# Pooled attention with a gated convolutional layer on one core: exponentials per head, division in two steps, two transposes of x by DMA, two conv quarters by taps, and a new order

## The chip, the core and the metric

The kernel runs on one core of a Trainium2 chip. Five engines work from queues of their own, each in order, and wait for each other by semaphores: TensorE (PE: matrix products and transposes), VectorE (DVE), ScalarE (ACT), GpSimd (POOL) and SyncE (SP, which here only starts transfers). Tensors lie in SBUF, on 128 partitions; products land in PSUM, which has eight banks of 512 fp32 values per partition. The metric is the device time of one execution in microseconds, lower is better.

## What is computed

q, k and v have 8 sequences, 8 heads, 576 positions and 64 values per head. Keys and values are averaged over 8 neighbouring positions, which leaves 72 per head; attention over these gives x, 576 x 512 per sequence. Then a layer with 1024 inner channels, a convolution of width 3 along the positions as the gate, and an output product:

```python
def _attn_ref(q, k, v):
    k_p = k.reshape(B, H, Sp, pool, D).mean(axis=3)
    v_p = v.reshape(B, H, Sp, pool, D).mean(axis=3)
    scores = scale * np.matmul(q, k_p.transpose(0, 1, 3, 2))
    scores = scores - np.max(scores, axis=-1, keepdims=True)
    attn = np.exp(scores)
    attn = attn / (np.sum(attn, axis=-1, keepdims=True) + 1e-09)
    return np.matmul(attn, v_p).astype(np.float32)

def _moe_ref(x, w_in, conv_w, w_out):
    h = np.maximum(x @ w_in, 0.0)
    ...
    for k in range(K):
        conv_out += conv_w[k][None, None, :] * hp[:, k:k + S, :]
    gate = 1.0 / (1.0 + np.exp(-conv_out))
    return (h * gate @ w_out).astype(np.float32)
```

The subtraction is of the maximum of each position and head, so it is one number per partition for each block of 72 scores.

## The kernel before

**Tiles.** Two sequences form a group (0 to 3). A group's 1152 positions make nine tiles of 128 (group 0: ten, since its sequences are kept apart), 37 in all. A tile (g, t) goes through one chain of operations, written in `add_att` (L1193):

- `att_scores` (TensorE): the scores of 8 heads, 8 x 72 columns, into two PSUM banks. The ring "s" has two slots, so at most two tiles' scores stand at once.
- `att_max` (VectorE, L608): the negated maximum per position and head, 8 columns "negm".
- `att_shift`: for groups 1 to 3 VectorE adds the negated maximum to all 576 scores and writes "sd" in SBUF (L620); for group 0 (`SHIFT_PE`) TensorE adds it within PSUM (L628). With that the scores' banks are free in groups 1 to 3.
- `att_exp` (ScalarE, L646): one exponential over all 576 columns, with the scale 1/64 for the mean over 8 and the root of 64.
- The exponentials "e" are transposed to "eT": by TensorE and a copy (`att_turn`, L657, `att_copy`, L671) in groups 0 and 1, by a DMA that SP starts (`att_send`, L666) in groups 2 and 3.
- `att_values` (TensorE, L682): products with the pooled values and a column that gives the sum.
- `att_divide` (VectorE): a reciprocal of the 8 sums (L695) and one multiplication over 512 columns (L697), which gives "x".
- x is transposed to "xT": for sequences below `X_DMA` by TensorE and a copy (`att_turn_out`, L714, `att_copy_out`, L722), for the others by a DMA that SP starts (`att_out`, L706).

**The layer** of a sequence b is `add_ffn` (L1246): for each of 8 blocks of 128 inner channels `ffn_in` (TensorE, L727, two halves of four matmuls into two PSUM banks) and `ffn_relu` (ScalarE, L736), which frees them. The convolution runs by groups of four blocks, (b, f4) with f4 = 0 or 1, which are called quarters here as in the change (a quarter of the two sequences of a group). Normally a quarter is two `ffn_conv` of two blocks on TensorE with diagonal weights (L889), four tanh on ScalarE (L914), `ffn_gate` (L925, L927) and a multiplication with h (`ffn_times`, L935) on VectorE. A sequence in `WRAP` has its ends copied by GpSimd first (`ffn_wrap`, L811 and L812), and an `ffn_conv` of it has 24 matmuls, else 32. For a quarter in `TAPS` no matmul is made: per block ScalarE multiplies h by the middle tap's weight, a scale per partition (L862), VectorE adds the two other taps (L864), ScalarE takes the tanh (L869), and `ffn_tap_gate` (L875, L876) gates all four blocks. The output products are `ffn_out` (TensorE, L943), a copy (`ffn_copy`, L954) and a store (`ffn_store`, L966).

**The order.** Every operation is listed once with its engines and a booked cost; the table `ORDER` gives the sequence in which they are issued. An entry n stands for operation n // 2, on its first engine if n is even and on its second if odd; -1 is a filler matmul at the start. `FORMS` and `PLACES` give the form of some products and the PSUM banks. So nothing is decided at run time: each engine works its list from top to bottom, and what stands behind a waiting operation waits too.

Of the kernel before, what the change touches and what calls it, by code (L numbers as in the profile page):

```python
# [33 lines left out]
class Graph:  # L34
# [20 lines left out]
    X_DMA = 4  # L55
# [3 lines left out]
    WRAP = (4, 5, 6, 7)  # L59
    TAPS = ((4, 1), (5, 0), (5, 1), (6, 0), (6, 1), (7, 0))  # L60
# [6 lines left out]
    SHIFT_PE = ((0, 0), (0, 1), (0, 2), (0, 3), (0, 4), (0, 5), (0, 6), (0, 7), (0, 8), (0, 9))  # L67
    TURN_DMA = 2
    BANKS = 8
    ORDER = (  # L70
# [52 lines left out]
    )  # L123
    FORMS = (
        1, 0, 1, 0, 1, 1, 1, 0, 0, 0, 0, 1, 1, 0, 0, 1, 1, 0, 0, 0, 0, 1, 1, 0, 0, 0, 0, 1, 0, 0, 0, 1, 1, 1, 1, 0, 1, 1, 1, 1,
    )
    PLACES = (
# [50 lines left out]
def kernel(  # L178
# [73 lines left out]
    def buf(*key):  # L252
        return buffers[key[0]][tokens[key].slots[0]]
# [1165 lines left out]
```

## Time and profile before

| | |
|---|---|
| median of 3 runs | 217.81 us (217.51 to 218.0) |
| span of the profiled execution, first to last instruction | 216.5 us |
| mean granted TensorE clock | 0.992 |
| data moved | 33.46 MB, mean 155 GB/s |
| DMA issued by SP for x (L706) / for e (L666) | 18 / 18 |

In the views an engine is PE, PEld (weight loads), DVE, ACT or POOL, and L12 is line 12 of the kernel. A group's row gives the operation, the tile written and read, shapes, count, then after the first bar the busy time in us and the mean of one in ns, and after the second the idle time before it with what ended it. Busy time of an engine counts overlapped stretches once: consecutive operations of ScalarE overlap at their ends, so a mean is longer than the distance between two starts. In a timeline or a chain the first number is the start, the second the length, both in us.

### The profile page before, as it was taken

How to read it: one execution, taken by the hardware profiler on the slowest of the kernel's cores; microseconds unless marked ns; L12 is line 12 of the kernel's file. 1: busy time of each engine (PE TensorE's matmuls, PEld its weight loads, DVE VectorE, ACT ScalarE, POOL GpSimd, SP SyncE). 2: the span in 40 equal slices, each digit the busy share in tenths (PEclk: the TensorE clock that was granted, in tenths of full speed). 3: DMA queues.
4: the chain of work that ended last, by engine and by line, in shares of the span. 5: the costliest groups of instructions: out<-in, count | busy, mean ns of one | idle time of the engine just before them, and what ended most of it. 6: DMA issues, size and time to landing. Idle time of an engine off the chain costs nothing.

```text
span 216.5 us, 6617 instructions
## 1 busy us (share of the span) xinstructions
PE 201.9 (93%) x2753; PEld 137.0 (63%) x2753; DVE 193.2 (89%) x334; ACT 162.7 (75%) x278; POOL 41.5 (19%) x78
## 2 busy tenths in 40 slices
PE   7599999969999999999999899989999999999992
PEld 3557778855788776766776675665656666654451
DVE  7598989999999999999999799999899999998621
ACT  2548885896998887787497594878979999997420
POOL 8644330050052101000000030002201210370000
PEclk9799999999999999999999999999999999999999
DMA  6999999999999999969687634576347745602685
GB/s 210 227 207 209 206 207 208 210 205 206 207 205 206 154 153 179 158 164 165 131 111 100 136 74 89 58 156 148 78 104 153 158 100 123 145 0 51 169 242 171
DMA packets 48833, 33.46 MB, mean 155 GB/s; under 512 B 28300, under 2 KB 43812, under 8 KB 48804
## 3 DMA queue, kind: packets, MB, share of 16 engines
q0 software_dynamic: 15216, 15.40, 43.5%
q1 hardware_dynamic: 32512, 16.13, 36.6%
q10 hardware_dynamic: 1076, 1.52, 2.5%
q8 instruction: 21, 0.34, 0.7%
q14 instruction: 8, 0.07, 0.1%
HBM read 32.52 MB, written 9.44 MB: 194 GB/s over the span
## 4 chain that ended last, share of the span: by engine, by line
PE 45%; DVE 34%; issue 6%; ACT 6%; DMA 5%; SPq 2%; DVEq 0%
PE psum L943 20%; PE psum L727 16%; DVE negm L608 7%; DVE x L697 6%; DVE sd L620 4%; DVE gT L935 4%; DMA hT<-in_k_dram 3%; DVE v L486 3%; DVE gT L927 3%; PE psum L889 2%; DMA out_dram<-osb 2%; DVE r L695 2%; PE psum L682 2%; ACT e L646 2%; DVE gT L925 1%
## 5 line engine op out<-in xcount | busy, mean ns | idle before, releaser
L727 PE MATMUL psum<-xT,w_in_sb 128*128 128x288 bf16 x512 | 74.1, 286 | 2.2 <-DMA xT<-x 1.1
L943 PE MATMUL psum<-w_out_sb,gT 128*128 128x512 bf16 (+1 forms) x296 | 69.5, 374 | 0.7 <-DVE gT L935 0.6
L727 PEld LDWEIGHTS <-w_in_sb 128*128 128x128 bf16 x512 | 47.9, 98 | 19.1 <-issue 2.0
L736 ACT ACTIVATE hT<-psum 128x576 bf16<-128x576 f32 x64 | 40.3, 650 | 14.0 <-PE psum L727 13.4
L943 PEld LDWEIGHTS <-gT 128*128 128x128 bf16 x296 | 27.3, 98 | 26.5 <-issue 0.9
L864 DVE SCALAR_TENSOR_TENSOR tg<-hT,convw,tg 128x576 f32<-128x576 bf16 x48 | 37.6, 815 | 0.5
L608 DVE TENSOR_REDUCE negm<-psum 128x8 f32<-128x576 f32 (+2 forms) x37 | 27.5, 752 | 2.3 <-PE psum L582 1.6
L697 DVE TENSOR_TENSOR x<-psum,r 128x512 bf16<-128x512 f32 (+1 forms) x37 | 25.6, 691 | 1.4
L811 POOL COPY hT<-hT 128x126 bf16<-128x126 bf16 x16 | 7.5, 467 | 97.6 <-ACT hT L736 80.1
L620 DVE TENSOR_TENSOR sd<-psum,negm 128x576 f32<-128x576 f32 x27 | 20.2, 753 | 0.5
L682 PE MATMUL psum<-vm,eT 128*128 128x130 bf16 (+5 forms) x240 | 18.9, 222 | 1.1 <-DVE x L697 0.7
L646 ACT ACTIVATE e<-sd 128x576 bf16<-128x576 f32 x27 | 18.2, 685 | 1.3 <-DVE sd L620 1.1
L954 ACT COPY osb<-psum 128x512 f32<-128x512 f32 x27 | 15.7, 585 | 4.4 <-PE psum L943 4.2
L889 PE MATMUL psum<-hT,dw 64*64 64x288 bf16 (+2 forms) x608 | 18.7, 261 | 0.1
L682 PEld LDWEIGHTS <-eT 128*128 128x128 bf16 (+1 forms) x240 | 15.3, 100 | 5.4 <-DMA eT<-e 1.2
L862 ACT ACTIVATE tg<-hT,convw 128x576 f32<-128x576 bf16 x24 | 18.1, 772 | 0.1
L889 PEld LDWEIGHTS <-dw 64*64 64x64 bf16 x608 | 14.8, 107 | 4.6 <-issue 3.7
L869 ACT ACTIVATE gT<-tg 128x576 bf16<-128x576 f32 x24 | 16.3, 683 | 0.7 <-DVE tg L864 0.5
L914 ACT ACTIVATE gT<-psum 128x576 bf16<-128x576 f32 x20 | 12.9, 651 | 3.9 <-PE psum L889 2.7
L914 ACT ACTIVATE tg<-psum 128x576 bf16<-128x576 f32 x20 | 13.0, 652 | 2.6 <-PE psum L889 1.4
L935 DVE TENSOR_TENSOR gT<-gT,hT 128x2304 bf16<-128x2304 bf16 x10 | 13.5, 1352 | 0.1
L486 DVE TENSOR_TENSOR v<-v 128x1280 bf16<-128x1280 bf16 (+2 forms) x24 | 13.0, 540 | 0.2
(84 smaller groups left out, 234.2 us busy)
## 6 DMA issues: line engine op xcount, KB each, us to landing
out_dram<-osb SPq DMA_DIRECT2D x54, 128.0 KB, 2.4
v<-in_v_dram POOLq DMA_DIRECT2D x8, 512.0 KB, 13.1
qp<-in_q_dram POOLq DMA_DIRECT2D x7, 576.0 KB, 14.4
kk<-in_k_dram POOLq DMA_DIRECT2D x3, 1152.0 KB, 14.6
out_dram<-qp ACTq DMA_DIRECT2D x10, 128.0 KB, 2.7
hT<-in_k_dram SPq DMA_DIRECT2D x2, 576.0 KB, 5.0
w_in_sb<-in_moe_w_in_dram POOLq DMA_DIRECT2D x2, 512.0 KB, 14.2
w_out_sb<-in_moe_w_out_dram POOLq DMA_DIRECT2D x1, 1024.0 KB, 24.7
```

Of the source, the lines that this page charges most:

```text
L608: nc.vector.tensor_reduce(out=a["m"][0:rows], in_=a["s"][0:rows, :, 0:2 * KW].rearrange("p a (h s) -> p a h s", s=Sp), axis=AX.X, op=OP.ma ...
L620: nc.vector.tensor_tensor(out=a["d"][0:rows], in0=a["s"][0:rows, :, 0:2 * KW].rearrange("p a (h s) -> p a h s", s=Sp), in1=a["m"][0:rows]. ...
L646: nc.scalar.activation(out=dst, in_=src, func=ACT.Exp, scale=1.0 / (POOL * 8.0),)
L682: nc.tensor.matmul(out=a["o"][lo:hi, h // 4, (h % 4) * (D + 1):(h % 4 + x1 - x0) * (D + 1)], lhsT=a["eT"][:, j, lo:hi], rhs=buf("vm", b)[: ...
L697: nc.vector.tensor_tensor(out=a["x"][0:rows].rearrange("p (a h d) -> p a h d", a=2, d=D), in0=ov[:, :, :, 0:D], in1=r[0:rows].unsqueeze(3) ...
L727: nc.tensor.matmul(out=banks(ps)[:, j, 0:SC], lhsT=w_in_block(dc, fb), rhs=buf("xT", g)[:, dc, i * S + j * SC:i * S + (j + 1) * SC], start ...
L736: nc.scalar.activation(out=h_of(b)[:, fb].rearrange("p (a s) -> p a s", a=2), in_=banks(ps)[:, :, 0:SC], func=ACT.Relu, scale=0.5,)
L864: nc.vector.scalar_tensor_tensor(out=acc, in0=h, scalar=w, in1=acc, op0=OP.mult, op1=OP.add)
L889: nc.tensor.matmul(out=banks(pss[r ^ c])[c * D:(c + 1) * D, j, lo:hi], lhsT=dw[r * D:(r + 1) * D, tap * n_fb + fb, :], rhs=hT[r * D:(r + 1 ...
L914: nc.scalar.activation(out=t.rearrange("p (a s) -> p a s", a=2), in_=banks(ps)[:, :, 0:SC], func=ACT.Tanh, scale=0.5,)
L935: nc.vector.tensor_tensor(out=gate, in0=gate, in1=h_of(b)[:, four], op=OP.mult)
L943: nc.tensor.matmul(out=bank(ps)[0:rows, columns], lhsT=buf("gT", g)[:, fb, t * P:t * P + rows], rhs=w_out_sb[:, fb, columns], start=(fb == 0),
```

## The change

- `EIGHT` lists all 27 tiles of groups 1 to 3. For these `att_shift` is left out, and `att_exp` issues eight activations, one per head, which read the 72 scores in PSUM and add the head's negated maximum as a bias per partition. The scale goes into the pooling matrix and the identity with which keys are turned (`KSCALE`), so `att_exp` has no scale any more.
- `att_divide` becomes `att_invert` (reciprocal, VectorE) and `att_divide` on either engine: one multiplication on VectorE, or eight activations with a scale per partition on ScalarE. In the new order 9 of 37 are on ScalarE: (0,2), (0,4), (1,3), (1,7), (2,1), (2,8), (3,1), (3,5), (3,6).
- `X_DMA` = 2: the nine tiles of group 1 have x transposed by DMA.
- `TAPS` gains (4,0) and (3,1); `WRAP` gains sequence 3. The gate of a taps quarter is listed as two operations.
- The late output buffers of group 3 wait for the q transfers of sequences 4 to 7, not for 7 alone.
- `ORDER`, `FORMS` and `PLACES` are new throughout. In the counts: copies of xT 15 on ScalarE and 4 on VectorE become 8 and 2; eT 16 and 3 become 12 and 7; whole-tile output copies 32 and 3 become 27 and 8; qT 7 and 7 become 9 and 5.

```diff
-    X_DMA = 4
+    X_DMA = 2
...
-    WRAP = (4, 5, 6, 7)
-    TAPS = ((4, 1), (5, 0), (5, 1), (6, 0), (6, 1), (7, 0))
+    WRAP = (3, 4, 5, 6, 7)
+    TAPS = ((4, 0), (4, 1), (5, 0), (5, 1), (6, 0), (6, 1), (7, 0), (3, 1))
...
+    KSCALE = 1.0 / (POOL * 8.0)
...
+    def by_head(g, t):
+        return (g, t) in Graph.EIGHT
...
-        nc.vector.memset(pm[0:TB, :, 0:Sp], 1.0)
+        nc.vector.memset(pm[0:TB, :, 0:Sp], KSCALE)
...
+        nc.vector.tensor_scalar(out=ident_k, in0=ident, scalar1=KSCALE, scalar2=None, op0=OP.mult)
...
+        if by_head(g, t):
+            for n in range(H):
+                r, k = n // 4, n % 4
+                at = (k // 2 * 4 + r * 2 + k % 2 if a["by_rows"] else n) * Sp
+                nc.scalar.activation(
+                    out=e[0:rows, at:at + Sp],
+                    in_=a["s"][0:rows, r, k * Sp:(k + 1) * Sp],
+                    func=ACT.Exp,
+                    bias=a["m"][0:rows, r, k:k + 1],
+                )
+            return
...
-            scale=1.0 / (POOL * 8.0),
...
+    def att_invert(g, t):
+        nc.vector.reciprocal(out=buf("r", g, t)[0:rows_of(g, t)], in_=att_heads(g, t)[:, :, :, D])
+
+    def att_divide(g, t, engine):
...
+        if engine == "ACT":
+            for n in range(H):
+                nc.scalar.activation(
+                    out=a["x"][0:rows, n * D:(n + 1) * D],
+                    in_=ov[:, n // 4, n % 4, 0:D],
+                    func=ACT.Identity,
+                    scale=r[0:rows, n // 4, n % 4:n % 4 + 1],
+                )
+            return
...
+        if by_head(g, t):
+            o = add({"ACT": 0.9}, key, lambda: att_exp(g, t), after=[o], uses=[e, s, ng, lim])
+        elif shift_by_dve(g, t):
...
-        o = add(dve(0.2, 0.69), key, lambda: att_divide(g, t), after=[o], uses=[x, rr, big])
+        o = add({"DVE": 0.115}, key, lambda: att_invert(g, t), after=[o], uses=[rr, big])
+        o = add({"DVE": 0.61, "ACT": 0.82}, key, None, after=[o], uses=[x, rr, big])
+        o.emit = lambda o=o: att_divide(g, t, o.engine)
```

More of the change, by code (lines that the diff above doesn't have):

```diff
@@ L67 @@
     SHIFT_PE = ((0, 0), (0, 1), (0, 2), (0, 3), (0, 4), (0, 5), (0, 6), (0, 7), (0, 8), (0, 9))
+    EIGHT = ((1, 0), (1, 1), (1, 2), (1, 3), (1, 4), (1, 5), (1, 6), (1, 7), (1, 8), (2, 0), (2, 1), (2, 2), (2, 3), (2, 4), (2, 5), (2, 6), (2, 7), (2, 8), (3, 0), (3, 1), (3, 2), (3, 3), (3, 4), (3, 5), (3, 6), (3, 7), (3, 8))
     TURN_DMA = 2
@@ L70 @@
     ORDER = (
[52 rows of a table removed]
[54 rows of a table added]
     )
     FORMS = (
-        1, 0, 1, 0, 1, 1, 1, 0, 0, 0, 0, 1, 1, 0, 0, 1, 1, 0, 0, 0, 0, 1, 1, 0, 0, 0, 0, 1, 0, 0, 0, 1, 1, 1, 1, 0, 1, 1, 1, 1,
+        0, 0, 1, 1, 1, 1, 1, 1, 1, 1, 1, 1, 0, 1, 1, 1, 1, 0, 0, 1, 0, 0, 0, 0, 0, 0, 1, 1, 0, 0, 0, 1, 1, 1, 1, 1, 1, 0, 1, 0,
     )
     PLACES = (
[17 rows of a table removed]
[16 rows of a table added]
     )
@@ L224 @@
     ident = const.tile([P, P], BF16, name="ident")
+    ident_k = const.tile([P, P], BF16, name="ident_k")
     mask = const.tile([P, NJ, 3], BF16, name="mask")
@@ L375, in build_pick @@
                     out=pick[:, hh].rearrange("p (s f a e) -> p s f a e", s=2, f=2, a=2)[:, :, f],
-                    in_=ident.rearrange("p (s a hh f e) -> p s a hh f e", s=2, a=2, hh=2, f=2)[:, :, :, hh, f],
+                    in_=ident_k.rearrange("p (s a hh f e) -> p s a hh f e", s=2, a=2, hh=2, f=2)[:, :, :, hh, f],
                 )
@@ L470, in turn_keys @@
                     lhsT=buf("kk", g)[:, c, 0:D],
-                    rhs=ident[:, i * D:(i + 1) * D],
+                    rhs=ident_k[:, i * D:(i + 1) * D],
                     start=True,
@@ L689, in att_values, with att_heads @@
                 )
-    def att_divide(g, t):
+    def att_heads(g, t):
+        return att[g, t]["o"][0:rows_of(g, t), :, 0:4 * (D + 1)].rearrange("p a (h d) -> p a h d", d=D + 1)
+    def att_invert(g, t):
+        nc.vector.reciprocal(out=buf("r", g, t)[0:rows_of(g, t)], in_=att_heads(g, t)[:, :, :, D])
+    def att_divide(g, t, engine):
         a, rows = att[g, t], rows_of(g, t)
-        ov = a["o"][0:rows, :, 0:4 * (D + 1)].rearrange("p a (h d) -> p a h d", d=D + 1)
-        r = buf("r", g, t)
-        nc.vector.reciprocal(out=r[0:rows], in_=ov[:, :, :, D])
+        ov, r = att_heads(g, t), buf("r", g, t)
         a["x"] = buf("x", g, t)
+        if engine == "ACT":
[7 more added lines that the diff above has]
+            return
         nc.vector.tensor_tensor(
@@ L872, in ffn_tap_gate @@
         g, i = where[b]
-        four = slice(4 * f4, 4 * f4 + 4)
-        gate = buf("gT", g)[:, four, i * S:(i + 1) * S]
+        gate = buf("gT", g)[:, 4 * f4:4 * f4 + 4, i * S:(i + 1) * S]
         nc.vector.tensor_scalar(out=gate, in0=gate, scalar1=1.0, scalar2=None, op0=OP.add)
-        nc.vector.tensor_tensor(out=gate, in0=gate, in1=h_of(b)[:, four], op=OP.mult)
     def ffn_conv(b, f2, pss):
@@ L1113, in add_pair @@
             t = token("ps", n=2)
-            o = add({"PE": 0.26}, key, lambda b=b, t=t: turn_keys(b, t), after=[prev, c0], uses=[t, kk[g]], mode=HALF, count=36)
+            o = add({"PE": 0.26}, key, lambda b=b, t=t: turn_keys(b, t), after=[prev, picked], uses=[t, kk[g]], mode=HALF, count=36)
             c = add(either(0.76, 0.71), key, None, after=[o], uses=[t, ktok[b]])
@@ L1209, in add_att @@
         o = add(dve(0.75), key, lambda: att_max(g, t), after=[o], uses=[ng, s])
-        if shift_by_dve(g, t):
+        if by_head(g, t):
+            o = add({"ACT": 0.9}, key, lambda: att_exp(g, t), after=[o], uses=[e, s, ng, lim])
+        elif shift_by_dve(g, t):
             sd = token("sd", g, t)
@@ L1292, in add_ffn @@
                 tanh.append(add(act(0.65 if Graph.ACC < 2 else 0.683), w, lambda fb=fb, ps=ps: ffn_tap_tanh(b, fb, ps), after=[o], uses=[ps, gtok[g]]))
-            gated = add(dve(0.78, 1.39), w, lambda f4=f4: ffn_tap_gate(b, f4), after=tanh, uses=[htok[b], gtok[g]])
+            o = add(dve(0.78), w, lambda f4=f4: ffn_tap_gate(b, f4), after=tanh, uses=[gtok[g]])
+            gated = add(dve(1.39), w, lambda f4=f4: ffn_times(b, f4), after=[o], uses=[htok[b], gtok[g]])
             gdone.setdefault(b, []).append(gated)
@@ L1326, in add_ffn @@
             if f2 % 2 and cross:
-                gated = add(dve(0.78, 1.39), w + 6 * f2 + Graph.GATE, lambda f4=f4: ffn_tap_gate(b, f4), after=tanh[f4], uses=[htok[b], gtok[g]])
+                o = add(dve(0.78), w + 6 * f2 + Graph.GATE, lambda f4=f4: ffn_tap_gate(b, f4), after=tanh[f4], uses=[gtok[g]])
+                gated = add(dve(1.39), w + 6 * f2 + Graph.GATE, lambda f4=f4: ffn_times(b, f4), after=[o], uses=[htok[b], gtok[g]])
                 gdone.setdefault(b, []).append(gated)
@@ L1340, in add_out @@
             key += nudge("ot", 9 * g + t)
-            osb, free = (token("late", g, t), qdone[7, 0]) if g == 3 else (token("osb", g, t), [])
+            osb, free = (token("late", g, t), [x for n in range(4, B) for x in qdone[n, 0]]) if g == 3 else (token("osb", g, t), [])
             need = [a for x in groups[g][0:i + 1] for a in gdone[x]]
```

139 rows, old and new, of tables (ORDER, PLACES) are left out of this document.

## The prediction

> **What bounds the kernel now.** I read the summary first, then the busy time by stretches, then the chain of work that ended last, and only then the groups and the timeline of ScalarE. Summary and chain by engine, from the page:
>
> ```profile
> span 216.5 us, 6617 instructions
> ...
> PE 201.9 (93%) x2753; PEld 137.0 (63%) x2753; DVE 193.2 (89%) x334; ACT 162.7 (75%) x278; POOL 41.5 (19%) x78
> ...
> PE 45%; DVE 34%; issue 6%; ACT 6%; DMA 5%; SPq 2%; DVEq 0%
> ```
>
> The same by stretches of the span (length, then busy time of PE, PEld, DVE, ACT, POOL, then clock, DMA share, GB/s):
>
> ```profile
> 0.00:20.00 20.00, 15.66 (x251) 10.21 (x252) 14.81 (x44) 10.50 (x18) 12.06 (x27) 0.91 1.05 213
> 20.00:50.00 30.00, 27.44 (x553) 21.87 (x554) 28.10 (x51) 23.51 (x40) 7.53 (x11) 1.00 1.23 207
> 50.00:144.00 94.00, 91.24 (x1461) 65.49 (x1457) 90.75 (x158) 74.36 (x128) 9.67 (x17) 1.00 0.89 147
> 144.00:200.00 56.00, 55.33 (x442) 33.42 (x442) 53.55 (x74) 50.25 (x86) 12.28 (x24) 1.00 0.49 108
> 200.00:216.50 16.50, 12.25 (x65) 6.04 (x63) 5.93 (x10) 4.05 (x8) 0.00 (x0) 1.00 0.68 191
> ```
>
> And pieces of the chain that ended last (start, length, what):
>
> ```profile
> 31.02 0.63 PE psum L657 x10
> ...
> 82.91 0.74 PE psum L889 x32
> ...
> 91.75 0.76 DVE sd L620
> ...
> 93.07 0.68 DVE negm L608
> ...
> 162.07 1.96 PE psum L727 x16
> 164.03 0.86 PE psum L943 x4
> ...
> 195.55 0.86 PE psum L889 x24
> ...
> 199.10 13.16 PE psum L943 x68
> ```
>
> TensorE and VectorE share the bound: the chain is mostly VectorE up to about 144 us and TensorE alone after it. ScalarE is third. Its idle time is 54 us, but not all of it is usable: 9.5 us lies in the first 20 us (20 - 10.50) and 12.45 us after 200 us (16.5 - 4.05), where the last output matmuls run. That leaves some 32 us, and only 20.6 us of it lies between 50 and 144 us (94 - 74.36).
>
> **The change, part by part.** Groups of instructions with their mean (busy us, mean ns):
>
> ```profile
> L620 DVE TENSOR_TENSOR sd<-psum,negm 128x576 f32<-128x576 f32 x27 | 20.2, 753 | 0.5
> L646 ACT ACTIVATE e<-sd 128x576 bf16<-128x576 f32 x27 | 18.2, 685 | 1.3 <-DVE sd L620 1.1 <-ACT osb L954 0.2
> L727 PE MATMUL psum<-xT,w_in_sb 128*128 128x288 bf16 x512 | 74.1, 286 | 2.2 <-DMA xT<-x 1.1 <-ACT tg L914 0.3 <-ACT gT L914 0.3
> L736 ACT ACTIVATE hT<-psum 128x576 bf16<-128x576 f32 x64 | 40.3, 650 | 14.0 <-PE psum L727 13.4
> L697 DVE TENSOR_TENSOR x<-psum,r 128x512 bf16<-128x512 f32 x35 | 24.2, 692 | 1.3
> L864 DVE SCALAR_TENSOR_TENSOR tg<-hT,convw,tg 128x576 f32<-128x576 bf16 x48 | 37.6, 815 | 0.5
> L954 ACT COPY osb<-psum 128x512 f32<-128x512 f32 x27 | 15.7, 585 | 4.4 <-PE psum L943 4.2
> L722 ACT COPY xT<-psum 128x512 bf16<-128x512 bf16 x13 | 7.6, 591 | 1.0 <-PE psum L714 0.6 <-DVE r L695 0.4
> L722 ACT COPY xT<-psum 128x256 bf16<-128x256 bf16 x2 | 0.7, 371 | 0.0
> L671 ACT COPY eT<-psum 128x640 bf16<-128x640 bf16 x14 | 9.5, 696 | 1.6 <-PE psum L657 1.5
> L534 ACT COPY qT<-psum 128x1152 bf16<-128x1152 bf16 x5 | 5.5, 1124 | 1.7 <-PE psum L520 1.7
> L671 DVE COPY eT<-psum 128x640 bf16<-128x640 bf16 x3 | 1.5, 484 | 0.4 <-ACT kT L431 0.4
> L954 DVE COPY qp<-psum 128x512 f32<-128x512 f32 x3 | 2.1, 689 | 6.0 <-PE psum L943 6.0
> L534 DVE COPY qT<-psum 128x1152 bf16<-128x1152 bf16 x5 | 3.8, 758 | 1.3 <-PE psum L520 1.3
> L927 DVE TENSOR_SCALAR gT<-tg 64x1152 bf16<-64x1152 bf16 x20 | 9.7, 485 | 0.3
> L925 DVE TENSOR_SCALAR gT<-gT 128x1152 bf16<-128x1152 bf16 x10 | 5.4, 542 | 0.0
> L875 DVE TENSOR_SCALAR gT<-gT 128x2304 bf16<-128x2304 bf16 x6 | 4.6, 772 | 0.9 <-ACT gT L869 0.9
> ```
>
> The term that decides is **one short biased ScalarE operation**; the trace has none of 72 columns. So I take it apart by the timeline of ScalarE (start, length of the merged piece, what):
>
> ```profile
> 74.19 1.61 ACT L458 CAST kT<-psum 64x288 bf16<-64x288 f32 x4
> ...
> 153.62 1.74 ACT L736 ACTIVATE hT<-psum 128x576 bf16<-128x576 f32 x3 [0.40 <-PE psum L727]
> ...
> 169.66 1.05 ACT L954 COPY osb<-psum 128x512 f32<-128x512 f32 x2
> ...
> 177.07 0.68 ACT L869 ACTIVATE gT<-tg 128x576 bf16<-128x576 f32 x1
> 177.64 1.43 ACT L862 ACTIVATE tg<-hT,convw 128x576 f32<-128x576 bf16 x2
> 178.97 0.67 ACT L869 ACTIVATE gT<-tg 128x576 bf16<-128x576 f32 x1
> ```
>
> - Slope: (591 - 371)/256 columns of L722 = 0.86 ns per column; I use 0.84, since from there to L671's 640 columns it is (696 - 591)/128 = 0.82. 72 columns take 0.060 us, 64 take 0.054.
> - Start to start from PSUM: three ReLUs (L736) in 1.74 us, the last 0.65 long, are 0.545 apart; less 504 columns (0.423) a 72-column operation would start every 0.122 us.
> - A per-partition operand: L862 reads its scale from a column of convw, L869 does not. 177.07 to 177.64 is 0.57; the two L862 start (178.97 - 177.64)/2 = 0.665 apart. So **0.095 us per operation goes to the operand, and 480 ns of streaming in the operation before did not hide it**.
>
> One biased exponential: 0.122 + 0.095 = 0.217 us; eight of them 1.74 us per tile in place of 0.57 (an exponential of 0.685 with its end overlapped, as L869). One 64-column division: 0.210; eight 1.68 us. Bounds: below, the operand hidden and the overhead of the two L954 copies, (1.05 - 0.585) = 0.465 less 440 columns (0.370) = 0.095, so 0.76 per tile and 0.70 per division; above, the four L458 casts, which hardly overlap: 0.405 apart, less 216 columns (0.181) and with the operand 0.319, so 2.55 and 2.5. I take 0.217: exponential and ReLU are the same kind, from PSUM to bf16.
>
> The Trainium skill, "ScalarE: Activation LUTs", section "What ACT_TABLE_LOAD costs", speaks against the change more strongly: 186 ns plus 0.833 ns per column, about 93 ns more per [128,1] operand, and 93 ns of overlap back to back. By it, as an estimate, an exponential starts every 0.247 us and the ScalarE total below would be 9 us higher; the operand's 0.095 of this trace agrees with it.
>
> ScalarE's queue, from 162.7 us:
> - 27 tiles of groups 1 to 3 (EIGHT): 27 x (1.74 - 0.57) = **+31.6**.
> - 9 divisions that the new ORDER gives to ScalarE (odd entries; seven of them in groups 1 to 3): 9 x 1.68 = **+15.1**. The other 28 stay on VectorE.
> - Quarters (4,0) and (3,1) by taps: 8 L862 of 0.665 = +5.3; their eight tanh move from PSUM to SBUF, +0.2.
> - Copies, each its mean less about 0.11 of overlap: xT 15 to 8 (-3.3), eT 16 to 12 (-2.3), output 32 to 27 (-2.4); qT 7 to 9 (+1.5, one of them short), start-up casts and kT about -0.6. Together -7.1.
>
> Sum 162.7 + 31.6 + 15.1 + 5.5 - 7.1 = **207.8 us**; 172.5 with the low bound, 237 with the high one.
>
> VectorE: 27 shifts -20.3, 9 multiplications -6.2, 16 taps +13.0, two gates 2 x (0.772 - 0.542 - 2 x 0.485) = -1.5, copies (eT +4, output +5, qT -2, xT -2) about +3: **-12 us**, to 181. The reciprocal is the same work in an instruction of its own. TensorE: 36 transposes of x at 0.063 (L657 is such a transpose: 10 in 0.63) -2.3; four conv pairs, two at 0.86 (24 matmuls) and two at 0.74 (32), -3.2; (3,0) goes from the 32 to the 24 form, +0.2: **-5.3 us**. GpSimd gets four more wraps and is 19% busy: cover ample, and without cover a wrap would hold the taps of its two blocks. The scaling moved into the pool matrix and the identities costs one small VectorE operation in the first microseconds: nothing.
>
> What is queued behind: ScalarE takes its list in order. Behind each train of eight stand ReLUs, which free the PSUM pairs of ffn_in; tanh and taps, which VectorE waits for; and, where ScalarE divides, the train waits for VectorE's reciprocal with all of that behind it. The scores' two PSUM banks, free before when the shift had read them, are held now until the eighth exponential, and at most two tiles are allowed (ring "s"). So a late ScalarE stops TensorE.
>
> **Sum.** The eight-fold trains begin with group 1, near 50 us, so the first 20 us and the run of output matmuls at the end keep their ScalarE idle time: 207.8 + 9.5 + 12.45 = **229.8 us** of span with no idle anywhere between. That is a floor for this price (20 to 50 us has 6.5 us of idle today, not all of which can be filled), while overlap at the ends of trains can give a little back; I keep it. The three runs' median 217.81 lies 1.3 us over the profiled span of 216.5, so **231 us**. By high and low neighbours of 0.217 (0.19 to 0.25, 288 operations): -7.8 to +9.5, so 223 to 240.
>
> **Rivals.**
> - *The short operations pack like copies, operand hidden: faster.* Place: the trains in ScalarE's queue; price 0.095 us per operation, ScalarE 172.5 us (80%), no bound. Then TensorE decides: its 5.3 us go, and of the 6.0 us that it idles from 20 to 200 us (180 - 174.0) perhaps 1.2, since VectorE has 12 us less: 216.5 - 6.5 + 1.3 = **211.3 us**. It decides below the price at which ScalarE just fits: (207.8 - (216.5 - 21.95))/288 = 0.046 less, with 3 us of idle left 0.057 less, so **0.16 us per operation**. For it: the two L954 copies come back to back at an overhead 0.027 us less than the ReLUs; the diff's own table books the eight at 0.9 us, which is a booking and no measurement. Against it: the L862 rows.
> - *Between:* at about 0.16 the gain on TensorE and the loss on ScalarE meet: **217 us**, same.
> - *Transposes by DMA come late.* Nine transfers of x join SP's queue between 50 and 100 us, where the engines' share is 0.89 against 0.49 later, ahead of stores and of the eT transfers. eT shows what late means:
>
> ```profile
> DMA to landing us min/median/max: 2.6/2.6/8.3
> ```
>
>   Sequences 3 and 2 would each wait once the 5.7 us of the worst over the median; on top of the fast case 211.3 + 11.4 = **223 us**. For it: L727 did wait for xT; against: it waited 1.1 us in all, with eighteen such transfers there already.
> - *Trains without any overlap* (0.319, as the casts): 237 + 22 + 1.3 = **261 us**. Against: those casts write half the partitions each; all else on ScalarE overlaps.
>
> **Chances.** ScalarE bound at 0.19 to 0.25: 0.50, 231 us, own range 223 to 240. Short operations packed: 0.36. Between: 0.05. Late DMA: 0.04. No overlap: 0.05. Range 209 to 239, which takes in both chief cases; they lie 20 us apart because one unmeasured price decides. What can be told from no change is about 0.2%: faster 0.38, same 0.03, slower 0.59.
>
> **What would show it.** Right: ScalarE above 95% busy between 50 and 170 us, the eight exponentials of a tile 0.2 us or more apart, TensorE idle before ffn_in with ScalarE as releaser, VectorE's busy time near 181 us. Wrong: exponentials starting every 0.1 to 0.15 us, ScalarE near 80% and TensorE over 94% busy.

## The result, and the profile after

The changed kernel is slower: ratio 1.1475 to the kernel before, 95% interval 1.1398 to 1.1553. Four runs gave 248.3, 251.02, 252.91 and 253.79 us (median 251.97) beside 217.66 us for the kernel before (217.51 to 218.0). The two highest of the four count as slow runs and are not in the ratio, so below **249.7 us**, the mean of the other two, stands for the changed kernel, and for u2 and u6, too, the time given is a single run, the faster of two, while the profile is that of the slower. The profiled execution of the changed kernel took 248.3 us, with a span of 246.6.

Summary, clock by slices and chain by engine, from its page:

```profile
span 246.6 us, 6716 instructions
...
PE 209.2 (85%) x2649; PEld 135.8 (55%) x2649; DVE 184.8 (75%) x317; ACT 202.8 (82%) x532; POOL 47.1 (19%) x86
...
PEclk9999999999998579996899999999999999999996
...
ACT 40%; PE 29%; DVE 15%; DMA 6%; issue 6%; SPq 1%; DVEq 0%; ACTq 0%
```

The chain has moved from PE and DVE (45 and 34% before) to ScalarE: 6% became 40%. But ScalarE's 202.8 us are 44 us less than the span. Where it idles is in the same stretches as before (length, busy time of PE, PEld, DVE, ACT, POOL, clock, DMA share, GB/s):

```profile
0.00:20.00 20.00, 13.76 (x238) 8.35 (x239) 14.84 (x45) 10.25 (x19) 9.47 (x20) 1.00 1.05 208
20.00:50.00 30.00, 27.51 (x620) 21.52 (x618) 24.76 (x48) 25.89 (x56) 8.31 (x15) 1.00 1.23 207
50.00:144.00 94.00, 80.11 (x1102) 54.53 (x1102) 66.58 (x115) 81.38 (x251) 12.78 (x22) 0.91 0.91 137
144.00:200.00 56.00, 48.54 (x431) 29.26 (x430) 45.89 (x70) 55.74 (x162) 6.42 (x16) 1.00 0.51 97
200.00:230.00 30.00, 28.84 (x209) 16.87 (x209) 28.50 (x38) 27.30 (x47) 10.12 (x14) 1.00 0.43 97
230.00:246.60 16.60, 10.49 (x56) 5.28 (x54) 4.23 (x6) 2.24 (x4) 0.00 (x0) 0.87 0.68 184
```

From 144 to 200 us ScalarE is busy 55.74 of 56 us: there it is the bound, as forecast. From 50 to 144 us **no engine** is: PE 80, ACT 81 and DVE 67 of 94 us. The rows of the new instructions, by shape:

```profile
L653 ACT ACTIVATE e<-psum,negm 128x72 bf16<-128x72 f32 x216 | 49.5, 414 | 2.0 <-DVE negm L616 2.0
L767 ACT ACTIVATE hT<-psum 128x576 bf16<-128x576 f32 x64 | 42.7, 711 | 5.6 <-PE psum L758 5.4
...
L721 ACT ACTIVATE x<-psum,r 128x64 bf16<-128x64 f32 x64 | 14.3, 382 | 3.3 <-DVE tg L895 2.1 <-DMA xT<-x 0.7 <-DVE r L713 0.5
```

A mean of 414 ns isn't the price of one: consecutive operations overlap, and single records run from 301 to 693 ns. The price is the distance of starts, on ScalarE's timeline:

```profile
69.18 1.74 ACT L721 ACTIVATE x<-psum,r 128x64 bf16<-128x64 f32 x8
70.76 0.70 ACT L767 ACTIVATE hT<-psum 128x576 bf16<-128x576 f32 x1
...
157.81 1.80 ACT L653 ACTIVATE e<-psum,negm 128x72 bf16<-128x72 f32 x8
159.45 0.64 ACT L983 COPY osb<-psum 128x512 f32<-128x512 f32 x1
```

Eight exponentials hold the queue for 159.45 - 157.81 = 1.64 us, **0.205 us each** (forecast 0.217); eight divisions for 1.58 us (forecast 1.68). Then the chain, where the stretch from 50 to 144 us lost time:

```profile
69.14 0.56 DVE x L728
69.72 8.78 DMA xT<-x
78.59 0.70 DVE x L728
...
88.55 3.79 PE psum L758 x16
...
103.96 4.06 DMA xT<-x
```

The transposes of x, now DMAs here, stand in it with 8.78 + 4.06 = 12.8 us; the exponentials (L653) have about 25% of the chain in this stretch, nearly twice as much. At 78.59 us VectorE's next division (L728) had waited until a DMA had read the buffer of an earlier x. What VectorE idled for this is less than the chain shows, since it had other work meanwhile: two such waits, 5.6 us in all. From issue to landing the 27 transfers of x took (first line), and the seven that were issued from 65 to 85 us, where the DMA share was about 1.2 (second line):

```profile
DMA to landing us min/median/max: 2.4/3.0/10.7
...
DMA to landing us min/median/max: 4.6/9.0/10.7
```

SP's queue was held by them, and then by a transfer of q, as its timeline shows (start, length):

```profile
65.59 20.33 SPq L737 DMA_TRANSPOSE xT<-x  x7
86.02 11.37 SPq L536 DMA_TRANSPOSE qT<-qp  x1
```

The 16 matmuls at 88.55 us took 0.237 us each; before, 16 took 1.96 us (162.07 us of the chain before), 0.1225 each. The granted clock is lower there, in two stretches of 20 us:

```profile
80.00:100.00 20.00, 17.00 (x189) 11.12 (x186) 12.86 (x24) 14.79 (x47) 1.77 (x2) 0.78 1.10 154
100.00:120.00 20.00, 16.62 (x234) 9.89 (x235) 14.31 (x23) 16.25 (x48) 5.05 (x10) 0.83 0.67 99
```

### The profile page after: what moved, and what is told of

Read it like the earlier page. It is cut to its first block, busy times and chain, and to the rows that moved or that the text cites. A ratio compares the mean times of both kernels' runs of the same rounds, so it can differ in the third digit from the quotient of the medians.

```text
span 246.6 us, 6716 instructions
## 1 busy us (share of the span) xinstructions
PE 209.2 (85%) x2649; PEld 135.8 (55%) x2649; DVE 184.8 (75%) x317; ACT 202.8 (82%) x532; POOL 47.1 (19%) x86
## 4 chain that ended last, share of the span: by engine, by line
ACT 40%; PE 29%; DVE 15%; DMA 6%; issue 6%; SPq 1%; DVEq 0%; ACTq 0%
ACT e L653 15%; PE psum L972 8%; PE psum L758 8%; DVE tg L895 6%; ACT hT L767 6%; DMA xT<-x 5%; ACT x L721 5%; PE psum L918 3%; ACT tg L893 3%; ACT gT L900 3%; ACT osb L983 2%; PE psum L700 2%; DVE gT L964 2%; PE psum L407 2%; DVE negm L616 2%
## 5 line engine op out<-in xcount | busy, mean ns | idle before, releaser
L895 DVE SCALAR_TENSOR_TENSOR tg<-hT,convw,tg 128x576 f32<-128x576 bf16 x64 | 50.1, 817 | 6.1 <-ACT tg L893 5.7
L653 ACT ACTIVATE e<-psum,negm 128x72 bf16<-128x72 f32 x216 | 49.5, 414 | 2.0 <-DVE negm L616 2.0
L767 ACT ACTIVATE hT<-psum 128x576 bf16<-128x576 f32 x64 | 42.7, 711 | 5.6 <-PE psum L758 5.4
L616 DVE TENSOR_REDUCE negm<-psum 128x8 f32<-128x576 f32 (+2 forms) x37 | 27.5, 755 | 14.8 <-PE psum L603 8.3
L700 PE MATMUL psum<-vm,eT 128*128 128x65 bf16 (+5 forms) x240 | 20.8, 230 | 6.2 <-ACT eT L689 3.2
L893 ACT ACTIVATE tg<-hT,convw 128x576 f32<-128x576 bf16 x32 | 25.6, 816 | 0.5
L728 DVE TENSOR_TENSOR x<-psum,r 128x512 bf16<-128x512 f32 (+1 forms) x28 | 19.1, 685 | 6.2 <-DMA xT<-x 5.6
L700 PEld LDWEIGHTS <-eT 128*128 128x128 bf16 (+1 forms) x240 | 16.4, 105 | 12.2 <-issue 5.3
L900 ACT ACTIVATE gT<-tg 128x576 bf16<-128x576 f32 x32 | 22.8, 726 | 0.0
L964 DVE TENSOR_TENSOR gT<-gT,hT 128x2304 bf16<-128x2304 bf16 x16 | 21.8, 1365 | 0.3
L721 ACT ACTIVATE x<-psum,r 128x64 bf16<-128x64 f32 (+1 forms) x72 | 16.0, 374 | 3.5 <-DVE tg L895 2.1
L713 DVE RECIPROCAL r<-psum 128x8 f32<-128x8 f32 (+1 forms) x37 | 7.5, 204 | 13.9 <-PE psum L700 7.6
L943 ACT ACTIVATE tg<-psum 128x576 bf16<-128x576 f32 x16 | 10.6, 663 | 3.7 <-PE psum L918 3.1
```

The costliest lines, as they stand in the source:

```text
L616: nc.vector.tensor_reduce(out=a["m"][0:rows], in_=a["s"][0:rows, :, 0:2 * KW].rearrange("p a (h s) -> p a h s", s=Sp), axis=AX.X, op=OP.ma ...
L653: nc.scalar.activation(out=e[0:rows, at:at + Sp], in_=a["s"][0:rows, r, k * Sp:(k + 1) * Sp], func=ACT.Exp, bias=a["m"][0:rows, r, k:k + 1],)
L700: nc.tensor.matmul(out=a["o"][lo:hi, h // 4, (h % 4) * (D + 1):(h % 4 + x1 - x0) * (D + 1)], lhsT=a["eT"][:, j, lo:hi], rhs=buf("vm", b)[: ...
L721: nc.scalar.activation(out=a["x"][0:rows, n * D:(n + 1) * D], in_=ov[:, n // 4, n % 4, 0:D], func=ACT.Identity, scale=r[0:rows, n // 4, n ...
L767: nc.scalar.activation(out=h_of(b)[:, fb].rearrange("p (a s) -> p a s", a=2), in_=banks(ps)[:, :, 0:SC], func=ACT.Relu, scale=0.5,)
L893: nc.scalar.activation(out=acc, in_=h, func=ACT.Identity, scale=w)
```

## The experiments

Theory A: ScalarE's added time is the loss, paid in full at the forecast price. Rival B: late transposes of x and a starved TensorE make the rest. Theory C in the expectations of u1 to u3 is TensorE's lower clock. Ratios are to the kernel before, run alongside (217.3 to 218.3 us); line numbers of a variant are its own. A letter u is a part undone in the changed kernel, v and x the kernel before with something put in, w the kernel before with VectorE relieved.

### Undoing one part

**u1**: all divisions on VectorE.

```diff
-        o.emit = lambda o=o: att_divide(g, t, o.engine)
+        o.emit = lambda o=o: att_divide(g, t, "DVE")
```

> The changed kernel with its nine ScalarE divisions back on VectorE. Theory A (ScalarE is the bound and its trains of eight set the price): ScalarE's busy time falls from 202.8 by 9 x 1.68 = 15 us, VectorE's rises by 6 us to 191, and the time falls by 8 to 15 us to 233 to 240 us. Theory B (the transposes of x by DMA in group 1 decide, VectorE and ScalarE wait for their buffers): the 12.8 us of DMA in the chain stay, and the time falls by less than 5 us, 243 us or more. Theory C (the lower granted clock of TensorE between 60 and 120 us decides): no change within 3 us.

240.56 us, ratio 1.1039 [1.0942, 1.1136]: 9 us back for 13.2 us of ScalarE (202.8 to 189.6 busy).

**u2**: the shift on VectorE again, right behind the maximum, and one exponential of 576 columns.

```diff
+        if by_head(g, t):
+            a["d"] = buffers["sd"][len(shifted) % 3]
+            shifted.append((g, t))
+            nc.vector.tensor_tensor(
...
+                op=OP.add,
+            )
...
-        if by_head(g, t):
+        if False:
```

> The changed kernel with the eight exponentials of groups 1 to 3 undone: VectorE shifts directly behind the maximum, one exponential per tile. Theory A: ScalarE loses 27 x 1.17 = 31 us (to 171), VectorE gains 20 us (to 205) and becomes the bound with TensorE: 220 to 230 us. Theory B: the late transposes stay, 235 us or more. Theory C: 245 us.

243.18 us; a miss. ScalarE fell to 176.1 us busy and VectorE rose to 201.8, and only 6.5 us came back. This alone does not show that ScalarE is not all of the loss: in the profile of this run ScalarE waits 17.2 us, 16 times, for the new shift, so VectorE took over a part of it.

**u3**: six of group 1's nine x tiles get buffers of their own (the unused "sd"), so that their divisions do not wait for a DMA to read an old x.

```diff
-        a["x"] = buf("x", g, t)
+        a["x"] = x_own[t] if g == 1 and t < 6 else buf("x", g, t)
```

> The changed kernel with six of the nine x tiles of group 1 in buffers of their own (the space of the shifted scores, unused there), so that no division waits for a transfer of an earlier x. Theory A alone: 245 to 250 us, the waits of VectorE for the transfer of xT (5.6 us) go and come back as waits for ScalarE. Theory B: the chain loses its 12.8 us of DMA, 235 to 240 us. Theory C: if the low clock follows from the stalls, the clock near 90 us returns to 1.00 and the time falls by more than the waits, below 235 us.

246.03 us, 1.129 [1.1247, 1.1332]: 3.6 us. One wait of 4.0 us for a transfer of x is left, and another wait came up at the next transfer of the same queue, as the waits of this run show (what waited, for what: total us, times, longest), while ScalarE idled 12.2 us between 50 and 144 us as before:

```profile
PE psum L702 <- DMA eT<-e: 7.2, 1, 7.2
```
```profile
50.00:144.00 94.00, 74.93 (x1105) 53.30 (x1113) 67.57 (x116) 81.80 (x256) 12.81 (x22) 0.96 0.94 140
```

**u4**: the eight exponentials keep their place and lose their bias.

```diff
-                    bias=a["m"][0:rows, r, k:k + 1],
```

> The changed kernel with the eight exponentials but without their bias: the maximum is computed and not subtracted. Theory A with 0.095 us for the operand: exponentials start every 0.12 us instead of 0.21, ScalarE's busy time falls by 216 x 0.095 = 20 us to 182, and the time to 228 to 235 us. If the operand costs nothing in short operations, spacing and time stay within 2%.

233.95 us, 1.0735 [1.0704, 1.0767]: 15.7 us back for 18.3 us of ScalarE (184.5 busy), so 0.085 us for each of 216 operands. Its timeline has sixteen in one piece:

```profile
158.02 2.04 ACT L653 ACTIVATE e<-psum 128x72 bf16<-128x72 f32 x16
159.78 0.76 ACT L982 COPY osb<-psum 128x512 f32<-128x512 f32 x1
```

1.76 us for 16 is 0.110 each without the operand (forecast 0.122), against 0.205 with it.

**u5**: group 1's x turned by TensorE again, with the copy on VectorE.

```diff
+        if g == 1:
+            turn = psum[:, FREE[t], :].bitcast(BF16).rearrange("p (j t) -> p j t", t=P)
+            for dc in range(n_dmc):
+                nc.tensor.transpose(
...
+            nc.vector.tensor_copy(out=buf("xT", g)[:, :, columns_of(g, t)], in_=turn[:, 0:n_dmc, 0:rows])
+            return
```

> The changed kernel with the x of group 1 turned by TensorE into a free PSUM bank and copied by VectorE, as in the kernel before, all else as changed. Theory B: the waits for transfers of xT between 65 and 110 us go, the clock of TensorE stays up, and the time falls by 10 to 18 us to 232 to 240 us, near the 231 us of the prediction, which had only ScalarE's price in it. Theory A alone: within 5 us of the changed kernel, 245 us or more.

245.9 us, 1.1253 [1.113, 1.1376]: 3.8 us, though no x of group 1 goes by DMA any more. This suggests that the late transposes lie mostly beside the trains of eight while these stand in ScalarE's queue.

### One part alone in the kernel before

**v1**: only the eight exponentials; the shift is left out, the old order stays.

```diff
+            for n in range(H):
+                r, k = n // 4, n % 4
...
+                nc.scalar.activation(
+                    out=e[0:rows, at:at + Sp],
+                    in_=a["s"][0:rows, r, k * Sp:(k + 1) * Sp],
+                    func=ACT.Exp,
+                    bias=a["m"][0:rows, r, k:k + 1],
+                )
+            return
```

> The kernel before, its order kept, with only the eight biased exponentials for the 27 tiles of groups 1 to 3, issued where the shift on VectorE stood (and the scale moved into the pooling matrix). Theory A: exponentials start 0.21 us apart, ScalarE's busy time rises from 163 by about 31 to 194 us; of this some 20 us find idle time between 50 and 144 us, so 225 to 232 us. Rival (a lighter VectorE pays for it): 214 to 219 us.

239.45 us, 1.0958 [1.0878, 1.1037]. ScalarE has 28.5 us more (191.2), VectorE 16 less (177.3), and the time is 21.2 us longer. Busy times from 50 to 144 us and two of the waits:

```profile
50.00:144.00 94.00, 79.70 (x1232) 57.70 (x1232) 63.74 (x113) 83.38 (x247) 7.75 (x14) 1.00 0.79 131
```
```profile
DVE negm L611 <- PE psum L585: 15.6, 10, 3.9
DVE r L710 <- PE psum L697: 15.4, 15, 2.5
```

ScalarE keeps 10.6 us of idle time there, and VectorE, relieved, waits 31 us in the whole span for scores and products of TensorE. TensorE in its turn waits for ScalarE: 8.9 us for the exponentials (3.7 of it in front of the next scores, whose PSUM they hold) and 10.2 us for its other operations. The clock is 1.00 in this stretch, so the loss there needs no throttle.

**v2**: only group 1's x by DMA.

```diff
+        if g == 1 and xtok[g].slots is not None:
+            att[g, t]["sent"] = True
+            att_out(g, t)
+            return
```

> The kernel before, its order kept, with only the x of sequences 2 and 3 transposed by DMA instead of TensorE and a copy. Theory B: the nine transfers fall into the stretch in which the loads of k, q and v fill the DMA engines, land after up to 10 us, and a division or an ffn_in waits for them: 225 to 235 us. Rival (the transfers are hidden, as forecast in the sum): 214 to 218 us, TensorE 2 us less busy.

229.12 us, 1.0485 [1.0408, 1.0562]: **10.9 us** lost by this part alone. A piece of its chain, the landing times of all 27 transfers of x and of the first seven (issued from 61.5 to 80.5 us), what waited for them, and TensorE after it:

```profile
66.95 0.43 DVE negm L608
67.38 12.28 DMA xT<-x
79.65 0.03 issue
```
```profile
DMA to landing us min/median/max: 2.4/2.5/12.3
...
DMA to landing us min/median/max: 2.5/4.0/12.3
...
DVE x L697 <- DMA xT<-x: 6.9, 3, 3.9
```
```profile
76.00:80.00 4.00, 2.90 (x20) 1.78 (x20) 2.20 (x5) 0.65 (x1) 0.00 (x0) 0.50 1.19 132
80.00:84.00 4.00, 3.29 (x55) 2.36 (x55) 2.12 (x5) 2.74 (x6) 1.23 (x1) 0.50 0.48 71
```

The chain shows one late transfer of 12.28 us, but the idle time is that of three waits of VectorE, 6.9 us in all; TensorE starved behind them and then had half its clock for these 8 us.

**v3**: only the nine divisions on ScalarE.

```diff
+        if (g, t) in ((0, 2), (0, 4), (1, 3), (1, 7), (2, 1), (2, 8), (3, 1), (3, 5), (3, 6)):
+            for n in range(H):
+                nc.scalar.activation(
...
+                    func=ACT.Identity,
+                    scale=r[0:rows, n // 4, n % 4:n % 4 + 1],
+                )
+            return
```

> The kernel before, its order kept, with only nine of the 37 multiplications of the division on ScalarE, the same nine tiles as in the changed kernel. ScalarE's busy time rises by 9 x 1.68 = 15 us to 178, VectorE's falls by 6 us. Theory A: this fits ScalarE's idle time only in part, since each train delays the ReLUs behind it: 218 to 224 us. Rival: hidden, 215 to 218 us.

228.82 us, 1.0471 [1.0311, 1.0632], more than I expected: 13.6 us more on ScalarE (176.3) cost 10.6 us, with ScalarE idle for more than 50 us of the span and VectorE 5 us lighter.

### Is ScalarE's idle time usable? Is VectorE a bound?

**v4 and x1**: per tile of groups 1 to 3 nine (v4) or four (x1) small copies behind the exponential, whose result nothing reads.

```diff
+        if shift_by_dve(g, t):
+            for n in range(9):
+                nc.scalar.copy(out=ident_2, in_=mask_wide[:, n % NJ, n % 3])
```

> The kernel before with nine short copies that nothing reads behind each exponential of groups 1 to 3, on ScalarE, 64 columns each and without an operand: 9 x 0.12 = 1.1 us per tile, 30 us in all, as much as the eight exponentials added. If occupied time in ScalarE's queue is what costs, whatever it computes: 235 to 243 us, as with the eight exponentials alone (239.5). If the exponentials' own lateness or the held PSUM banks cost: below 228 us.

279.68 us, 1.2813 [1.2778, 1.2848]. The dose was mis-sized; the timeline has the reason:

```profile
102.58 2.44 ACT L654 COPY ident<-mask_wide 128x64 bf16<-128x64 bf16 x9
```

Nine took 2.44 us, 0.27 each, with no overlap. I put it down to their writing one and the same tile; this was not tested apart from their reading SBUF. ScalarE got 54.1 us more (216.8), the time 61.6 us, at a mean clock of 0.929.

> The kernel before with four short copies that nothing reads behind each exponential of groups 1 to 3, 0.27 us each as the nine took: 27 x 1.09 = 29.5 us more in ScalarE's queue. If each microsecond there costs 0.93 as with nine copies (61.6 us for 66): 243 to 247 us. If the idle time of 20 us between 50 and 144 us takes its share first: 226 to 232 us.

232.33 us, 1.0675 [1.0632, 1.0718]: 21.1 us more on ScalarE, 14.9 us longer, at full clock and with no other engine touched. At this dose added ScalarE time is paid at 0.7, although this is the third engine of the kernel. (By the time that four copies hold the queue, 94.96 to 95.93 us on its timeline, it is 26 us more and a price of 0.57.)

```profile
PE 203.6 (88%) x2753; PEld 136.7 (59%) x2753; DVE 194.8 (85%) x334; ACT 183.8 (80%) x386; POOL 40.5 (18%) x78
```

**w1**: the opposite: in groups 1 to 3 one maximum per position over all heads, one exponential of 576 columns with that as bias, no shift.

```diff
+        if shift_by_dve(g, t):
+            a["m"] = buf("negm", g, t)[:, 0:1]
+            nc.vector.tensor_reduce(
...
+            nc.scalar.activation(out=dst, in_=src, func=ACT.Exp, bias=a["m"][0:rows])
+            return
```

> The kernel before, its order kept, with one maximum per position over all eight heads and one biased exponential per tile in groups 1 to 3, at the place of the shift, which is gone. VectorE loses 20 us (to 173), ScalarE gains 27 x 0.07 = 2 us. TensorE, 93% busy, becomes the only bound: 210 to 215 us. If the old order holds VectorE's gain back: 215 to 218 us.

218.4 us, 1.003 [1.0003, 1.0056], nine runs. VectorE is 16 us lighter, ScalarE 1.4 heavier, and nothing is gained:

```profile
PE 201.5 (93%) x2753; PEld 136.2 (63%) x2753; DVE 177.0 (82%) x308; ACT 164.1 (76%) x278; POOL 42.0 (19%) x78
...
PE 68%; DMA 10%; DVE 9%; ACT 7%; issue 3%; POOL 0%; DVEq 0%; ACTq 0%
```

VectorE's 34% of the chain shrank to 9%, and TensorE, busy for 93% before and here, took 68%. So what the change takes off VectorE is worth nothing by itself in this order.

**x4 and x2**: w1 for all 37 tiles, which also takes group 0's shift off TensorE; x2 puts the copies of xT on VectorE besides.

```diff
-                            stop=(n == 3 and shift_by_dve(g, t)),
+                            stop=(n == 3),
...
-            scale=1.0 / (POOL * 8.0),
+            bias=a["m"][0:rows],
...
-            o.emit = lambda o=o: att_copy_out(g, t, copier(o))
+            o.emit = lambda o=o: att_copy_out(g, t, nc.vector.tensor_copy)
```

> As x2 but with the copies of xT where they were: only TensorE's ten shifts of group 0 (about 2.5 us) and VectorE's 27 are gone. If TensorE's time counts one to one: 215 to 216.5 us. If the start hides it: 217 to 218.5 us.

220.27 us, 1.0106 [1.007, 1.0142].

> The kernel before with one maximum per position over all heads and one biased exponential in all 37 tiles, so without any shift on VectorE or TensorE, and with all copies of xT on VectorE. ScalarE 7 us less, TensorE 3 us less, VectorE 14 us less. If ScalarE's queue is paid in both directions: 209 to 213 us. If TensorE alone bounds: 215 to 217 us.

222.69 us, 1.0234 [1.0175, 1.0293]. Neither gains. A likely reason, not shown, is the fixed order: work taken off an engine doesn't let the others go earlier, and what is put elsewhere in the lists delays them.

### Taking several parts back

**u6**: w1's maximum and single exponential in the changed kernel, and u1's divisions.

```diff
-            for n in range(H):
...
+            nc.scalar.activation(out=dst, in_=src, func=ACT.Exp, bias=a["m"][0:rows])
...
-        o.emit = lambda o=o: att_divide(g, t, o.engine)
+        o.emit = lambda o=o: att_divide(g, t, "DVE")
```

> The changed kernel with its trains gone and nothing put on VectorE for them: in groups 1 to 3 one maximum per position over all eight heads (the same softmax, as a constant per row drops out) and one biased exponential over 576 columns, about 0.64 us; all divisions on VectorE. ScalarE's busy time falls to about 160 us. If ScalarE's queue was all of the loss: 208 to 214 us. If the transposes of x by DMA cost by themselves what they cost in the old order (11 us): 220 to 228 us.

232.97 us, with ScalarE at 163.6 us busy, as light as before the change. That is 1 us less than u4, which left ScalarE 21 us heavier: these 21 us cost next to nothing, and something else holds the kernel at about 233 us.

**u7**: u6 and, as in u5, group 1's x by TensorE, copied by ScalarE.

```diff
+            nc.scalar.copy(out=buf("xT", g)[:, :, columns_of(g, t)], in_=turn[:, 0:n_dmc, 0:rows])
```

> As the last, and the x of group 1 turned by TensorE with a copy on ScalarE. If both causes are named, taps and new order are left with light queues: 207 to 214 us. If it stays above 220 us, something else in the change (the two quarters by taps, the order itself) costs.

227.53 us, 1.0424 [1.0393, 1.0455]. The transposes of x are that something for 5.4 us (against the single run of u6). From 60 to 120 and from 120 to 200 us, the kernel before and then u7:

```profile
60.00:120.00 60.00, 57.89 (x1020) 42.94 (x1018) 58.50 (x105) 47.44 (x83) 5.84 (x9) 1.00 0.99 156
120.00:200.00 80.00, 78.82 (x751) 49.18 (x752) 75.84 (x111) 68.52 (x116) 15.49 (x32) 1.00 0.50 105
```
```profile
60.00:120.00 60.00, 51.70 (x808) 38.11 (x807) 47.59 (x85) 44.57 (x76) 10.63 (x20) 0.97 0.88 140
120.00:200.00 80.00, 76.93 (x783) 50.17 (x780) 78.06 (x119) 72.02 (x119) 15.87 (x28) 1.00 0.59 114
```

**u8**: u7's x and divisions, with u4's eight exponentials in place of the single one.

```diff
-                    bias=a["m"][0:rows, r, k:k + 1],
...
+            nc.scalar.copy(out=buf("xT", g)[:, :, columns_of(g, t)], in_=turn[:, 0:n_dmc, 0:rows])
...
+        o.emit = lambda o=o: att_divide(g, t, "DVE")
```

> The changed kernel with eight exponentials without bias (the maximum is computed, not subtracted; about 1.0 us per tile), all divisions on VectorE and the x of group 1 turned by TensorE with a copy on ScalarE. If price, divisions and DMA are the whole loss: 210 to 214 us, the faster branch of the forecast. If the two quarters by taps and the new order lose by themselves, as 227.5 us with one exponential per tile suggests: 226 to 234 us.

227.37 us, 1.0443 [1.0397, 1.0489], the same as u7. Trains at 0.110 us per operation cost no more than one exponential, although ScalarE is 7.5 us busier with them (175.2 against 167.7), and the kernel is still 10 us slower than before.

**x3**: w1, and two more quarters, (4,0) and (7,1), by taps in the old order, to see whether such quarters are the 10 us; (7,1) takes the place of the change's (3,1).

```diff
+    BY_TAPS = ((4, 0), (7, 1))
...
+        if (b, f2 // 2) in BY_TAPS:
+            return
...
+            acc = buffers["sd"][len(tapped) % 3].rearrange("p a h s -> p (a h s)").rearrange("p (a s) -> p a s", a=2)
```

> The kernel of one maximum per position in groups 1 to 3 (218.4 us), with quarters (4,0) and (7,1) by taps in place of the matmuls: ScalarE +5 us, VectorE +12 us (to 189), TensorE -3.4 us. If the taps cost through ScalarE's queue and VectorE's lateness: 221 to 226 us. If TensorE's relief counts: 214 to 217 us.

241.04 us, 1.1075 [1.1028, 1.1122]. Inconclusive: I had three accumulators for it, and the taps stand where the tanh stood, so ScalarE waits for VectorE, 18.4 us in all against 4.6 in the changed kernel (the largest of the waits of this run):

```profile
ACT gT L938 <- DVE sd L936: 15.7, 8, 3.2
```

## Why the prediction was wrong in its size

**Right: the price and the direction.** 0.205 us per biased exponential against 0.217, the operand 0.085 (u4's busy time) to 0.095 (0.205 - 0.110) against 0.095. The estimate of 0.247 us from the figures of the Trainium skill ("ScalarE: Activation LUTs", section "What ACT_TABLE_LOAD costs") was too high here: the rows decide. ScalarE came to 202.8 us against 207.8; 36 trains at 0.10 us less each are 3.6 of these 5. VectorE came to 184.8 against 181, and TensorE waited for ScalarE, as the forecast said it would: 22.3 us in all, 2.6 of them in front of ffn_in for exponentials.

**The step that failed: "207.8 + 9.5 + 12.45 = 229.8 with no idle anywhere between. That is a floor [...]; I keep it."** The floor was taken as the forecast. In the profile ScalarE idles 246.6 - 202.8 = 43.8 us, not 21.95. By the stretches above: 9.75 us up to 20, 4.1 to 50, **12.6 to 144**, 0.26 to 200, 2.7 to 230 and 14.4 to the end. So 229.8 - 5.0 of busy time + 21.85 of idle time = 246.6. The idle time inside was named (20.6 us before, between 50 and 144 us) and assumed to fill up; of those 94 us ScalarE was busy 81.38, and from 50 to 170 us 107.25 of 120, 89% where the prediction asked for over 95%. In the 94 us ScalarE waited 7.2 us for TensorE, 4.1 for VectorE and 1.0 for DMA. Only from 144 to 200 us did the list run without idle time, as the sum wanted it everywhere.

**Why it does not fill up.** The runs give what a microsecond more of ScalarE's busy time costs in the kernel before: 0.78 (v3), 0.74 (v1), 0.71 (x1), 1.14 (v4, at a lower clock); taken back from the changed kernel, 0.69 (u1) and 0.86 (u4). None of these is near zero, although x1 starts from 54 us of idle time. TensorE's waits, summed over the rows of each profile, show where it is paid. TensorE waits for ScalarE 0.8 us in the kernel before, and 9.9 us in v3, 14.8 in x1 and 19.1 in v1, which lost 10.6, 14.9 and 21.2 us. So most of the time is lost on TensorE, which is 93% busy and has no room: an operation behind the added ones comes later, and with it the PSUM or the input that TensorE needs next. For that reason the threshold of 0.16 us, "the price at which ScalarE just fits", was wrong as well: nothing had to overflow for a loss. The price is no constant, though. From u6 to u4 20.9 us of ScalarE cost 1.0 us, and from u7 to u8 7.5 us cost nothing: where something else already holds the kernel back, added time on ScalarE can be free.

**The rival "transposes by DMA come late" was right and was put in the wrong place.** Its price, 2 x 5.7 = 11.4 us, is close to what v2 lost alone (10.9), but by luck: it counted one wait for each of two sequences, and in v2 VectorE's divisions waited three times for the buffers of x, 6.9 us, with TensorE at half its clock behind. I gave it 0.04 and added it to the fast case only, as if ScalarE bound and late transfers excluded each other. They share the loss: 3.6 to 3.8 us come back while the trains stand (u3, u5), 5.4 us when they are gone (u6 to u7). The three parts alone make 21.2 + 10.9 + 10.6 = 42.7 us, the whole change 32.

**The faster branch** (0.36, 211.3 us) fails even at its own price: u8 pays 0.110 us per operation, has its divisions on VectorE and no late transposes in group 1, and takes 227.4 us. The branch counted on TensorE's 5.3 us and VectorE's 12; w1, x4 and x2 gained nothing from such relief in the old order.

**TensorE's clock** was not in the prediction. It falls to 0.78 and 0.83 where TensorE is starved (how, the last section shows). u3 raised its mean from 0.957 to 0.981 and won 3.6 us, while v1 lost 21 us and x1 15 us at 0.989 and 1.000, so these losses need no lower clock. In the changed kernel it adds (1 - 0.957) x 246.6 = 10.6 us at most, an estimate that takes TensorE as busy whenever the clock was low, against 1.7 us in the kernel before; how much of this counted was not separated.

**Open:** the 10 us that u7 and u8 keep. They still have two more quarters by taps and an order laid out for trains and transposes that are no longer there; x3 didn't tell these apart. From 120 to 200 us VectorE is busy 78.06 of 80 us in u7, so the taps may be the bound there. But of the 12.0 us by which TensorE idles longer in u7 than before, only 1.9 lie there and 6.2 from 60 to 120 us, where no engine is the bound; and TensorE still waits 8.3 us for ScalarE (0.8 before), though ScalarE is only 5 us busier. This speaks for the order rather than the taps; it is argued, not shown. No version tried was faster than the kernel before.

## What to carry to other kernels

In a kernel whose engines work fixed lists, idle time of the third engine isn't room while another engine is nearly full and waits for it: here added busy time cost 0.7 to 1.1 of itself, and nothing only where the kernel was already held back by something else. Take "busy time plus the idle ends" for a floor, never for the forecast. Before work is moved to relieve an engine, take that work away as a test: here 16 us off an engine at 89% gained nothing. Price each part alone, and do not let one loss rule out another: here the parts alone lost 42.7 us, and together, with the rest of the change, 32.

## What the runs showed of the hardware

- One [128,1] operand costs a 72-column activation 0.085 to 0.095 us, nearly as much as all the rest of it (0.110).
- Nine 64-column copies from SBUF into one and the same tile did not overlap and started 0.27 us apart, against 0.110 us for 72-column exponentials from PSUM that write side by side. Which of the differences does it was not tested.
- DMA transposes of x landed in 2.4 us at best and 12.3 us at worst. In v2 the first seven, at a DMA share of 1.2 from 60 to 80 us, took 2.5 to 12.3 us, the twenty later ones 2.4 to 4.0; in the changed kernel 4.6 to 10.7 and 2.4 to 7.6.
- The granted TensorE clock fell in the middle of the kernel. In stretches of 4 us of the changed kernel, at the end of the wait of 8.78 us for x and behind it:

```profile
76.00:80.00 4.00, 1.83 (x52) 1.40 (x53) 1.41 (x3) 2.46 (x7) 0.00 (x0) 0.82 1.36 188
80.00:84.00 4.00, 4.00 (x42) 2.37 (x38) 2.18 (x6) 3.12 (x12) 0.45 (x1) 0.50 0.90 111
```

  TensorE was busy 1.83 of 4 us, and when its work came it got half the clock, 0.50. The Trainium skill, "TensorE: Matmul & The Clock Gate", section "Part 1: The HAM clock gate", says that the clock halves after an idle window of some 3.4 us and comes back after a busy one. The trace agrees with the half, 0.50. It shows no stop of that length here: TensorE stood still for 1.63 us at most (77.71 to 79.34 us), and the clock fell within this time.
